# Converting a mixture's weights through a PSUM bank, with four word buffers

## The chip, the cores and the metric

The program runs on one core of a Trainium2 chip. Its engines are TensorE (PE, with its weight load PEld), VectorE (DVE), ScalarE (ACT), GpSimd (POOL) and SyncE (SP), which here issues nearly all input DMAs. The metric is the device time of one execution in microseconds (us): 1005.35 is the median of three runs before (1004.15 to 1005.42).

## The reference

Three layers in a row. A windowed attention: 4 batches, 8 heads, 768 positions of 64; a query sees the 128 positions up to its own and the first 4. A dense layer with three gates, and a routed layer of 8 experts:

```
x = softmax(where(keep, q@k.T/8, -1e9)) @ v          # then (3072, 512)
h = max(max(x@w1, x@w2), x@w3)                       # w*: (512, 768)
y = h @ w_out                                        # (768, 512)
out[tokens of e] = relu(y[tokens] @ u1[e]) @ u2[e]   # greedy routing, 384 tokens each
```

The weights w1, w2, w3, w_out come as 64-bit floats. All else is float32, and routing needs close to its full precision, so most products are computed from a high and a low part of each operand, in three matmuls.

## The kernel before

Work is cut into 8 groups of 384 tokens. A group needs four attention units (two heads each); the first 8 units, of groups 0 and 1, are "native", in plain float32. A unit is scores on PE (L123), copies and masks to a tile T (ACT L134, DVE L130 and L135 to L137), a row maximum (DVE L141), exponentials (ACT L144), a reciprocal and a scaling on POOL (L147), transposes on PE (L25), a mask product (DVE L163) and the product with v (PE L170, L172). A native unit needs key tiles with zeros in half of the partitions: `zeros` writes them (L53), into memory that the output weights take later.

`group` runs the first dense layer: six slices f of the hidden width, each 36 matmuls (L268, mm), whose maxima are taken by ACT and DVE (L270, L271) into hm; then a high and a low part of h are made (L275, L276). Group 0 is special: its slices are written to memory from hm (L278) and read back later by `reload`, which makes the parts again; the parts that `group` makes for it are not read.

The slices' weights must be converted first, 18 blocks of 128x512 for w1 to w3 and 6 for w_out. `single` loads 64-bit words into st (two buffers), DVE takes out bits of the low word into cA (L220), ACT scales the other word (L221), POOL adds the two (L222) and DVE puts in the sign and top bits (L223). `split` then makes the high part on ACT (L212) and the low part on POOL (L213). All of these tiles lie in SBUF. `load_w(f)` does this for the three blocks of one slice.

The order of each engine's instructions is fixed when the program is built, by a list scheduler that works with its own costs; the string `order` gives the sequence in which the units (a) and the weight slices (w) are offered to it. On the chip every engine runs its list in order, and a DMA queue does too.

Of the kernel before, what the change touches and what calls it, by code (L numbers as in the profile page):

```python
# [26 lines left out]
class Attn:  # L27
# [175 lines left out]
class Moe1:  # L203
    def __init__(s, tc, words,wgate, consts, wpool, main, conv, mm, pt, pss, ident):
        s.tc=tc; s.nc=tc.nc; s.mm=mm; s.pss=pss; s.main=main; s.conv=conv; s.ident=ident; s.consts=consts
        s.src=words; s.wgate=wgate
        s.W=[[wpool.tile([128,4,768],FR,name=f"w{i}{x}") for x in "hl"] for i in range(3)]
        s.WO=None; s.at=None
        s.WG=main.tile([128,6,16],FR,name="wgt")
    def split(s,src,hi,lo):  # L210
        nc=s.nc
        nc.scalar.activation(hi,src,AF.Copy)  # L212
        nc.gpsimd.tensor_tensor(lo,src,f32(hi),op=OP.subtract)  # L213
    def single(s,src):

        nc=s.nc
        st=s.conv.tile([128,512,2],I32,name="st",bufs=2)
        nc.sync.dma_start(st.rearrange("p n t -> p (n t)"),src.bitcast(I32))
        A=s.conv.tile([128,512],I32,name="cA",bufs=2); C=st[:,:,0]
        nc.vector.tensor_scalar(A,st[:,:,1],0x07ffffff,3,op0=OP.bitwise_and,op1=OP.logical_shift_left)  # L220
        nc.scalar.activation(C,st[:,:,0].bitcast(U32),AF.Copy,scale=2.0**-29)  # L221
        nc.gpsimd.tensor_tensor(A,A,C,op=OP.add)  # L222
        nc.vector.scalar_tensor_tensor(A,st[:,:,1],-0x40000000,A,op0=OP.bitwise_and,op1=OP.bitwise_or)  # L223
        return A.bitcast(FT)
    def load_w(s,f):
        for i in range(3):
            v=s.single(s.src[f*3+i]).rearrange("p (k n) -> p k n",k=4)
            s.split(v,s.W[i][0][:,:,f*128:(f+1)*128],s.W[i][1][:,:,f*128:(f+1)*128])
    def load_out(s,f):
# [17 lines left out]
        for x in range(2):  # L247
            nc.vector.tensor_copy(s.WO[x][:,f,:,256:260],f32(s.WG[:,f,8*x:8*x+8]).rearrange("p (u e) -> p u e",u=2))
    def group(s,xs,spill=None,pair=False,pool=None,mid=None,between=None):

        nc=s.nc; main=s.main
        X=[]
        for p in range(4):
# [4 lines left out]
            X.append((h,l))  # L258
        H=[]
        for f in range(6):  # L260
            if between is not None: between(f)
            m=main.tile([128,384],FT,name="hm",bufs=2)
            for i in range(3):
# [8 lines left out]
                if mid is not None and (f,i)==s.at: mid()  # L272
            h,l=((pool or main).tile([128,384],FR,name=f"h{x}{f}",bufs=1) for x in "hl")
            with s.tc.high_priority():
                nc.scalar.activation(h,m,AF.Copy)  # L275
                nc.vector.tensor_tensor(l,m,f32(h),op=OP.subtract)  # L276
            if spill is not None:
                for d,x in (zip(spill[f],(h,l)) if pair else ((spill[f],m),)): nc.sync.dma_start(d,f32(x))  # L278
            H.append((h,l))
# [243 lines left out]
class Moe2:  # L523

    def __init__(s,tc,w1,w2,x2d,out,wpool,act,main,mm,acc,pt,ident,nring):
        s.tc=tc; s.nc=tc.nc; s.w1=w1; s.w2=w2; s.x2d=x2d; s.out=out
        s.wp=wpool; s.act=act; s.main=main; s.ng=0; s.mm=mm; s.acc=acc; s.pt=pt; s.ident=ident; s.nring=nring
        s.scat=[]; s.n=-1
# [23 lines left out]
    def turn(s,xg,more=None):  # L552
# [9 lines left out]
        for d in range(4):  # L562
# [15 lines left out]
    def expert(s,X,ev,idx,mid=None):  # L578
# [9 lines left out]
        for f in range(F):  # L588
# [6 lines left out]
            h,l=(s.main.tile([128,384],FR,name=n%(4+f%2),bufs=1) for n in ("hh%d","hl%d"))  # L595
            with s.tc.high_priority():
# [13 lines left out]
def attention_mixtures(tc,q,k,v,vs,words,wg,u1,u2,out,off=60,spread=(0,1,3,4),native=8,order='a0 a0 a0 a0 w a1 a1 w w w w w a1 a1 a2',order1='a2 o o o o o o a2 a2',back=1,at=(1,0),s1=300,s2=400,nring=6):  # L610
    nc=tc.nc
    PS=bass.MemoryType.PSUM
    with ExitStack() as ctx:
# [19 lines left out]
        with tc.block(schedule_with_timeline_sim=True):  # L633
# [17 lines left out]
            for g in range(NG):  # L651
# [10 lines left out]
                if g==NG-1:  # L662
# [103 lines left out]
```

## Time and profile before

| | |
|---|---|
| median of 3 runs | 1005.35 us |
| profiled execution | 1004.42 us, of which its span is 1002.7 us |
| PE busy | 943.7 us, 94% |
| DVE, ACT, POOL busy | 711.8, 535.0, 343.5 us |
| mean granted clock of PE | 0.978 |

The busy share of PE is a mean over stages, so the stretches have to be read one by one. A busy PE is not a dense one: what a matmul costs in a row of matmuls is the distance between two starts, which is about half of the duration that its row shows.

### The profile page before, as it was taken

To read this page: it belongs to the slowest core of one execution; us is meant where nothing else is said; L and a number is where in the kernel's file an instruction comes from. 1 tells how busy PE (TensorE), PEld (TensorE's weight loads), DVE (VectorE), ACT (ScalarE), POOL (GpSimd) and SP (SyncE) were. 2 spreads that over 40 slices of the span, in tenths; PEclk is the share of its full clock that TensorE was granted. 3 is DMA by queue.
4 is the path that set the end of the run, shared out by engine and by line. 5 is a ranking of instruction groups with operands and counts; after the bars stand their busy time and mean duration, and the time that the engine had idled before them with its cause. 6 is when DMAs were issued, how large, how long until landed. Compare 5 with 4: busy or idle time off the path is not lost.

```text
span 1002.7 us, 18536 instructions
## 1 busy us (share of the span) xinstructions
PE 943.7 (94%) x6594; PEld 860.5 (86%) x6594; DVE 711.8 (71%) x1770; ACT 535.0 (53%) x1416; POOL 343.5 (34%) x307
## 2 busy tenths in 40 slices
PE   4879999979999999999999999989999999999996
PEld 3668899879999998998999998887888887888895
DVE  7988987787888875776754444887888988843320
ACT  5667664888878776677653211332433343454431
POOL 3687655044645435335433000011202111233331
PEclk9899999998999998999999999998999999999999
DMA  7444412231112111112210002542435443553430
GB/s 213 135 155 139 133 62 65 65 99 61 52 50 70 54 45 59 37 47 72 71 48 12 1 1 75 179 133 88 152 99 169 129 143 121 169 189 114 149 106 32
DMA packets 50541, 95.04 MB, mean 95 GB/s; under 512 B 6704, under 2 KB 20784, under 8 KB 50448
## 3 DMA queue, kind: packets, MB, share of 16 engines
q1 hardware_dynamic: 45312, 79.04, 25.5%
q0 software_dynamic: 3840, 12.45, 3.7%
q10 hardware_dynamic: 1296, 2.36, 0.6%
q8 instruction: 52, 0.85, 0.4%
q14 instruction: 41, 0.34, 0.1%
HBM read 77.84 MB, written 16.12 MB: 94 GB/s over the span
## 4 chain that ended last, share of the span: by engine, by line
PE 68%; DVE 13%; ACT 7%; issue 6%; DMA 4%; POOL 1%; POOLq 0%; DVEq 0%; SPq 0%; ACTq 0%
PE mm L268 24%; PE acc L587 11%; PE mm L594 11%; PE mm L291 6%; PE po L181 3%; PE rc L392 2%; PE pp L25 2%; DVE kz L95 1%; PE pt L25 1%; DMA sa<-in_u_dram 1%; PE ps L123 1%; DVE qs L97 1%; DMA st<-in_words_dram 1%; DMA sb<-in_u_dram 1%; DVE cA L223 1%
## 5 line engine op out<-in xcount | busy, mean ns | idle before, releaser
L177 POOL TENSOR_TENSOR L<-A_w,H 128x768 fp32r<-128x768 f32 x46 | 87.7, 1906 | 125.6 <-ACT H L176 101.2
L271 DVE TENSOR_TENSOR hm<-mm,hm 128x384 f32<-128x384 f32 x96 | 53.1, 553 | 53.9 <-PE mm L268 52.4
L549 POOL DMA_INDIRECT xg<-x2d,idx x24 | 25.5, 1063 | 188.5 <-PE mm L594 67.0
L537 ACT ACTIVATE wah<-sa 128x512 fp32r<-128x512 f32 x64 | 40.5, 632 | 89.6 <-PE mm L594 65.6
L537 ACT ACTIVATE wbh<-sb 128x512 fp32r<-128x512 f32 x64 | 40.4, 631 | 72.8 <-PE acc L587 61.5
L291 PE MATMUL mm<-woh,hh 128*128 128x260 f32 (+1 forms) x252 | 75.2, 300 | 4.2 <-DVE LG L294 4.2
L587 PE MATMUL acc<-wbh,hh 128*128 128x512 f32 x192 | 77.7, 404 | 0.0
L291 PE MATMUL mm<-woh,hl 128*128 128x260 f32 (+1 forms) x252 | 73.6, 296 | 4.2 <-DVE hl L308 2.7
L587 PE MATMUL acc<-wbh,hl 128*128 128x512 f32 x192 | 77.2, 402 | 0.0
L587 PE MATMUL acc<-wbl,hh 128*128 128x512 f32 x192 | 76.9, 401 | 0.0
L291 PE MATMUL mm<-wol,hh 128*128 128x260 f32 (+1 forms) x252 | 73.2, 292 | 0.0
L538 DVE TENSOR_TENSOR wbl<-sb,wbh 128x512 fp32r<-128x512 f32 x64 | 44.0, 688 | 35.0 <-ACT wbh L537 34.8
L268 PE MATMUL mm<-xh,w2h 128*128 128x384 f32 x192 | 67.3, 351 | 1.2 <-ACT hm L270 1.2
L268 PE MATMUL mm<-xh,w1h 128*128 128x384 f32 x192 | 67.0, 349 | 1.3 <-DVE hm L271 0.5
L268 PE MATMUL mm<-xh,w0h 128*128 128x384 f32 x192 | 66.9, 348 | 0.0
L268 PE MATMUL mm<-xl,w0h 128*128 128x384 f32 x192 | 65.3, 340 | 1.2 <-DVE xl L257 1.2
L268 PE MATMUL mm<-xl,w1h 128*128 128x384 f32 x192 | 65.5, 341 | 0.0
L268 PE MATMUL mm<-xh,w1l 128*128 128x384 f32 x192 | 65.3, 340 | 0.0
L268 PE MATMUL mm<-xl,w2h 128*128 128x384 f32 x192 | 65.3, 340 | 0.0
L268 PE MATMUL mm<-xh,w2l 128*128 128x384 f32 x192 | 65.2, 340 | 0.0
L268 PE MATMUL mm<-xh,w0l 128*128 128x384 f32 x192 | 64.7, 337 | 0.0
L598 DVE SCALAR_TENSOR_TENSOR hl<-mm,hh 128x384 fp32r<-128x384 f32 x64 | 35.3, 552 | 40.7 <-ACT hh L597 40.3
(315 smaller groups left out, 3087.1 us busy)
## 6 DMA issues: line engine op xcount, KB each, us to landing
sa<-in_u_dram SPq DMA_DIRECT2D x64, 256.0 KB
sb<-in_u_dram SPq DMA_DIRECT2D x64, 256.0 KB
st<-in_words_dram SPq DMA_DIRECT2D x24, 512.0 KB
qn<-in_q_dram SPq DMA_DIRECT2D x24, 192.0 KB
x2d<-xo SPq DMA_DIRECT2D x15, 256.0 KB
kn<-in_k_dram SPq DMA_DIRECT2D x12, 264.0 KB
vn<-in_v_dram SPq DMA_DIRECT2D x12, 256.0 KB
kn<-in_k_dram SPq DMA_DIRECT2D x12, 198.0 KB
```

The source lines that it names most:

```text
L25: nc.tensor.transpose(out,x,f32(ident))
L177: nc.gpsimd.tensor_tensor(L,Af,f32(H),op=OP.subtract)
L181: nc.tensor.matmul(po[:,q:q+n],u['VS'][:,blk,128*h:128*h+128],part[:,c:c+n],start=(part is H and j==0),stop=False,skip_group_check=True)
L268: nc.tensor.matmul(ps[:,:384],s.W[i][a][:,p,f*128:(f+1)*128],X[p][b],start=(n==0),stop=(n==11)); n+=1
L271: else: nc.vector.tensor_tensor(m,ps[:,:384],m,op=OP.max)
L291: nc.tensor.matmul(ps[:,:n],H[f][a][:,t*128:(t+1)*128],s.WO[b][:,f,u,:n],start=(k==0),stop=(k==17)); k+=1
L537: nc.scalar.activation(h,src,AF.Copy)
L538: (nc.gpsimd if s.n>=6 and nm=="wa" else nc.vector).tensor_tensor(l,src,f32(h),op=OP.subtract)
L549: nc.gpsimd.indirect_dma_start(out=g,out_offset=None,in_=s.x2d[0:first or 3072],in_offset=bass.IndirectOffsetOnAxis(ap=idx[:,t:t+1],axis=0 ...
L587: nc.tensor.matmul(acc[t],H[f][a][:,t*128:(t+1)*128],W[f][1][b],start=(f==0 and n==0),stop=(f==F-1 and n==2)); n+=1
L594: nc.tensor.matmul(ps[:,:384],W[f][0][a][:,k,:],X[k][b],start=(n==0),stop=(n==11)); n+=1
L598: nc.vector.scalar_tensor_tensor(l,ps[:,:384],0.0,f32(h),op0=OP.max,op1=OP.subtract)
```

## The change

`zeros` uses POOL in place of DVE. In `single` the bits of the low word go to a PSUM bank of the pool `ps`, which has three banks and also takes the scores; DVE then joins the top bits with them, into an SBUF tile R, and POOL adds the scaled word last. R is one of three tiles where A was one of two. For w1 to w3 (`ring`) the words go in turn to four buffers in one tile HL, which later holds the high and low parts of h and is used by group 0 for nothing else; w_out keeps the two buffers st. Group 0 writes hm to memory and makes no parts. Tiles that were single ones (hh0 to hl5) are slices of HL.

```diff
     def zeros(s,ts):
-        for h,t in enumerate(ts): s.nc.vector.memset((f32(t) if t.dtype==FR else t)[64-64*h:128-64*h],0.0)
+        for h,t in enumerate(ts): s.nc.gpsimd.memset((f32(t) if t.dtype==FR else t)[64-64*h:128-64*h],0.0)
...
-    def single(s,src):
+    def single(s,src,ring=False):
 
         nc=s.nc
-        st=s.conv.tile([128,512,2],I32,name="st",bufs=2)
+        if ring and s.stage is None: s.stage=s.main.tile([128,12,384],FT,name="HL").rearrange("p a b -> p (a b)").bitcast(I32)
+        if ring: st=s.stage[:,s.n%4*1024:(s.n%4+1)*1024].rearrange("p (n t) -> p n t",t=2)
+        else: st=s.conv.tile([128,512,2],I32,name="st",bufs=2)
         nc.sync.dma_start(st.rearrange("p n t -> p (n t)"),src.bitcast(I32))
-        A=s.conv.tile([128,512],I32,name="cA",bufs=2); C=st[:,:,0]
+        A=s.pss.tile([128,512],FT,name="ps").bitcast(I32); C=st[:,:,0]
+        if ring and s.n%3==2: R=s.stage[:,4096:4608]
+        else: R=s.conv.tile([128,512],I32,name="cA",bufs=2)
+        s.n+=1
         nc.vector.tensor_scalar(A,st[:,:,1],0x07ffffff,3,op0=OP.bitwise_and,op1=OP.logical_shift_left)
         nc.scalar.activation(C,st[:,:,0].bitcast(U32),AF.Copy,scale=2.0**-29)
-        nc.gpsimd.tensor_tensor(A,A,C,op=OP.add)
-        nc.vector.scalar_tensor_tensor(A,st[:,:,1],-0x40000000,A,op0=OP.bitwise_and,op1=OP.bitwise_or)
-        return A.bitcast(FT)
+        nc.vector.scalar_tensor_tensor(R,st[:,:,1],-0x40000000,A,op0=OP.bitwise_and,op1=OP.bitwise_or)
+        nc.gpsimd.tensor_tensor(R,R,C,op=OP.add)
+        return R.bitcast(FT)
+    def part(s,x,f):
+        return s.HL[:,"hl".index(x)*6+f]
...
         H=[]
+        if s.HL is None and spill is None: s.HL=main.tile([128,12,384],FR,name="HL")
...
-            h,l=((pool or main).tile([128,384],FR,name=f"h{x}{f}",bufs=1) for x in "hl")
+            if s.HL is None: nc.sync.dma_start(spill[f],m); continue
+            h,l=(pool.tile([128,384],FR,name=f"h{x}{f}",bufs=1) if pool else s.part(x,f) for x in "hl")
```

The scheduler then lists the work of the first half anew. The counts of the instructions are the same but for the ten memsets (from DVE to POOL) and six high and six low parts of 128x384 (gone from ACT and DVE). From the last slice of the seventh group's first layer on, PE's list is the same as before.

POOL near the start: T_w and wol are units' tiles T, vk_ and vns belong to a unit's first positions, cA and st (or HL) to the conversion. Before:

```order
L114 MEMSET T_w 128x264 x2
L114 MEMSET wol 128x264
L101 CAST vk_103<-vns 40x128
L102 TENSOR_TENSOR vk_103<-vns,vk_103 40x128
L101 CAST vk_107<-vns 40x128
L102 TENSOR_TENSOR vk_107<-vns,vk_107 40x128
L222 TENSOR_TENSOR cA<-cA,st 128x512 x2
L213 TENSOR_TENSOR w0l<-cA,w0h 128x4x128
L147 TENSOR_TENSOR T_w<-T_w,l 128x792
L222 TENSOR_TENSOR cA<-cA,st 128x512
L213 TENSOR_TENSOR w1l<-cA,w1h 128x4x128
```

In the changed kernel, where the eight memsets of L53 stand ahead of these rows:

```order
L114 MEMSET wol 128x264
L101 CAST vk_103<-vns 40x128
L102 TENSOR_TENSOR vk_103<-vns,vk_103 40x128
L101 CAST vk_107<-vns 40x128
L102 TENSOR_TENSOR vk_107<-vns,vk_107 40x128
L147 TENSOR_TENSOR T_w<-T_w,l 128x792
L114 MEMSET T_w 128x264
L101 CAST vk_103<-vns 40x128
L147 TENSOR_TENSOR T_w<-T_w,l 128x792
L102 TENSOR_TENSOR vk_103<-vns,vk_103 40x128
L147 TENSOR_TENSOR wol<-wol,l 128x792
L228 TENSOR_TENSOR cA<-cA,HL 128x512
```

The scalings (L147) of the first three units now stand in front of the first weight block (L228 is the addition, which was L222); before, two additions and a low part stood in front of the first scaling.

POOL later, where the weights of the fourth and fifth slices are made (w0l to w2l are the low parts). Before:

```order
L213 TENSOR_TENSOR w0l<-cA,w0h 128x4x128
L147 TENSOR_TENSOR wol<-wol,l 128x792
L213 TENSOR_TENSOR w1l<-cA,w1h 128x4x128
L222 TENSOR_TENSOR cA<-cA,st 128x512
L101 CAST vk_103<-vns 40x128
L222 TENSOR_TENSOR cA<-cA,st 128x512
L102 TENSOR_TENSOR vk_103<-vns,vk_103 40x128
L213 TENSOR_TENSOR w2l<-cA,w2h 128x4x128
L147 TENSOR_TENSOR T_w<-T_w,l 128x792
L114 MEMSET wol 128x264
L213 TENSOR_TENSOR w0l<-cA,w0h 128x4x128
L222 TENSOR_TENSOR cA<-cA,st 128x512
```

In the changed kernel:

```order
L101 CAST vk_107<-vns 40x128
L228 TENSOR_TENSOR HL<-HL 128x512
L213 TENSOR_TENSOR w1l<-cA,w1h 128x4x128
L228 TENSOR_TENSOR cA<-cA,HL 128x512
L102 TENSOR_TENSOR vk_107<-vns,vk_107 40x128
L213 TENSOR_TENSOR w2l<-HL,w2h 128x4x128
L228 TENSOR_TENSOR cA<-cA,HL 128x512
L213 TENSOR_TENSOR w0l<-cA,w0h 128x4x128
L228 TENSOR_TENSOR HL<-HL 128x512
L213 TENSOR_TENSOR w1l<-cA,w1h 128x4x128
L228 TENSOR_TENSOR cA<-cA,HL 128x512
L213 TENSOR_TENSOR w2l<-HL,w2h 128x4x128
```

Additions and low parts now follow each other almost without a unit's work between them.

PE, in the second slice of group 0's first dense layer (xh and xl are the parts of its tokens, w0h to w2l the weights, pt and pp transposes of a unit's T). Before:

```order
L123 MATMUL ps<-woh,qf 128x260 x3
L268 MATMUL mm<-xh_1043,w0h 128x384
L268 MATMUL mm<-xl_1044,w0h 128x384
L268 MATMUL mm<-xh_1043,w0l 128x384
L25 MATMUL pt<-ident,wol 128x128 x3
L25 MATMUL pp<-ident,wol 128x128 x3
L268 MATMUL mm<-xh_1047,w0h 128x384
L268 MATMUL mm<-xl_1048,w0h 128x384
L268 MATMUL mm<-xh_1047,w0l 128x384
L268 MATMUL mm<-xh_1051,w0h 128x384
L268 MATMUL mm<-xl_1052,w0h 128x384
L268 MATMUL mm<-xh_1051,w0l 128x384
```

In the changed kernel, in the same slice (L276 was L268):

```order
L276 MATMUL mm<-xh_1050,w1l 128x384
L276 MATMUL mm<-xh_1038,w2h 128x384
L276 MATMUL mm<-xl_1039,w2h 128x384
L276 MATMUL mm<-xh_1038,w2l 128x384
L276 MATMUL mm<-xh_1042,w2h 128x384
L276 MATMUL mm<-xl_1043,w2h 128x384
L276 MATMUL mm<-xh_1042,w2l 128x384
L276 MATMUL mm<-xh_1046,w2h 128x384
L276 MATMUL mm<-xl_1047,w2h 128x384
L276 MATMUL mm<-xh_1046,w2l 128x384
L276 MATMUL mm<-xh_1050,w2h 128x384
L276 MATMUL mm<-xl_1051,w2h 128x384
```

Slices of group 0 now follow each other, and the scores and transposes of the seventh unit on come later.

## Rows read from the trace of the kernel before

**Rows 1.** The page, part 1: busy us, share and instructions by engine.

```profile
PE 943.7 (94%) x6594; PEld 860.5 (86%) x6594; DVE 711.8 (71%) x1770; ACT 535.0 (53%) x1416; POOL 343.5 (34%) x307
```

**Rows 2.** Stretches: busy us of PE, PEld, DVE, ACT, POOL; PEclk; DMA share; GB/s.

```profile
0.00:75.00 75.00, 52.41 (x225) 38.92 (x225) 66.38 (x133) 46.32 (x164) 46.32 (x49) 0.91 0.55 167
...
117.00:200.00 83.00, 79.71 (x511) 77.14 (x510) 64.54 (x122) 53.46 (x142) 33.76 (x26) 0.99 0.23 72
...
545.00:1002.70 457.70, 439.29 (x3405) 386.15 (x3404) 288.95 (x962) 156.42 (x304) 74.99 (x71) 0.99 0.35 112
```

**Rows 3.** Shorter stretches, same columns.

```profile
20.00:30.00 10.00, 5.51 (x19) 4.46 (x19) 9.80 (x17) 7.12 (x26) 5.78 (x5) 0.67 0.66 202
...
50.00:75.00 25.00, 19.79 (x98) 15.47 (x94) 22.20 (x39) 16.57 (x59) 20.36 (x16) 0.93 0.49 155
```

**Rows 4.** Waits of PE, 0 to 75 us: total us, times, longest.

```profile
PE ps L123 <- DVE wol L135: 6.1, 3, 5.3
...
PE ps L123 <- DVE T_w L135: 4.8, 5, 2.0
```

**Rows 5.** Waits of the SP queue, 0 to 120 us, same columns.

```profile
SPq L218 <- DVE cA L223: 28.1, 13, 7.7
```

**Rows 6.** DVE by line, 0 to 170 us: busy us, mean ns, idle before.

```profile
L223 DVE SCALAR_TENSOR_TENSOR cA<-st,cA 128x512 int32<-128x512 int32 x24 | 28.4, 1181 | 1.3 <-POOL cA L222 1.2
L220 DVE TENSOR_SCALAR cA<-st 128x512 int32<-128x512 int32 x24 | 19.4, 811 | 2.5 <-DMA st<-in_words_dram 2.4
...
L163 DVE TENSOR_TENSOR A_w<-pp,ul 128x768 f32<-128x768 f32 x10 | 9.5, 950 | 1.7 <-PE pp L25 1.6
...
L276 DVE TENSOR_TENSOR hl<-hm,hh 128x384 fp32r<-128x384 f32 x9 | 8.3, 921 | 3.1 <-ACT hh L275 3.1
```

**Rows 7.** Line L223: ns min/median/max, first and last start in us.

```profile
L223 DVE SCALAR_TENSOR_TENSOR cA<-st,cA x24: 641/763/3184, 15.3 to 161.9; 128x512 int32<-128x512 int32 x24
```

**Rows 8.** Line L213, its third group, same columns.

```profile
L213 POOL TENSOR_TENSOR w2l<-cA,w2h x6: 1257/1284/1299, 30.4 to 115.7; 128x512 fp32r<-128x512 f32 x6
```

**Rows 9.** POOL by line, 0 to 170 us: busy us, mean ns, idle before.

```profile
L222 POOL TENSOR_TENSOR cA<-cA,st 128x512 int32<-128x512 int32 x24 | 34.0, 1420 | 17.4 <-DVE cA L220 7.8 <-ACT st L221 5.7 <-ACT m L142 1.8
L147 POOL TENSOR_TENSOR T_w<-T_w,l 128x792 f32<-128x792 f32 x7 | 11.5, 1646 | 1.3 <-DVE l L146 1.3
...
L102 POOL TENSOR_TENSOR vk<-vns,vk 40x128 fp32r<-40x128 f32 x12 | 7.6, 635 | 0.2
```

**Rows 10.** Timeline of DVE, 0 to 40 us: start us, us, instruction.

```profile
8.11 0.23 DVE L130 COPY_PREDICATED T_w<-ca,ps 128x128 f32<-128x128 uint8 x1
...
13.45 0.42 DVE L220 TENSOR_SCALAR cA<-st 128x512 int32<-128x512 int32 x1
...
32.19 1.98 DVE L220 TENSOR_SCALAR cA<-st 128x512 int32<-128x512 int32 x1
```

**Rows 11.** Timeline of POOL, 0 to 40 us, same columns.

```profile
1.04 0.56 POOL L114 MEMSET T_w<- 128x264 f32 x2
...
38.40 1.72 POOL L147 TENSOR_TENSOR wol<-wol,l 128x792 f32<-128x792 f32 x1 [1.47 <-DVE l L146]
```

**Rows 12.** Timeline of PE, 37 to 47 us, same columns.

```profile
37.90 0.89 PE L268 MATMUL mm<-xh,w0h 128*128 128x384 f32 x1
...
43.55 1.29 PE L172 MATMUL po<-wol,vnn 128*64 128x256 f32 x6
44.78 0.55 PE L25 MATMUL pp<-ident,wol 128*128 128x128 f32 x3
45.17 1.48 PE L123 MATMUL ps<-woh,qf 128*128 128x260 f32 x6
46.49 0.49 PE L25 MATMUL pp<-ident,wol 128*128 128x128 f32 x3
```

**Rows 13.** Timeline of PE, 100 to 120 us, same columns.

```profile
103.37 0.34 PE L268 MATMUL mm<-xh,w0h 128*128 128x384 f32 x1
103.55 0.33 PE L268 MATMUL mm<-xl,w0h 128*128 128x384 f32 x1
```

More of the change, by code (lines that the diff above doesn't have):

```diff
@@ L207, in __init__ @@
         s.W=[[wpool.tile([128,4,768],FR,name=f"w{i}{x}") for x in "hl"] for i in range(3)]
-        s.WO=None; s.at=None
+        s.WO=None; s.at=None; s.stage=None; s.HL=None; s.n=0
         s.WG=main.tile([128,6,16],FR,name="wgt")
@@ L248, in load_out, with group @@
             nc.vector.tensor_copy(s.WO[x][:,f,:,256:260],f32(s.WG[:,f,8*x:8*x+8]).rearrange("p (u e) -> p u e",u=2))
-    def group(s,xs,spill=None,pair=False,pool=None,mid=None,between=None):
+    def group(s,xs,spill=None,pool=None,mid=None,between=None):
         nc=s.nc; main=s.main
@@ L277, in group @@
             if spill is not None:
-                for d,x in (zip(spill[f],(h,l)) if pair else ((spill[f],m),)): nc.sync.dma_start(d,f32(x))
+                for d,x in zip(spill[f],(h,l)): nc.sync.dma_start(d,f32(x))
             H.append((h,l))
@@ L305, in reload @@
             nc.sync.dma_start(m,spill[f])
-            h=s.main.tile([128,384],FR,name=f"hh{f}",bufs=1); l=s.main.tile([128,384],FR,name=f"hl{f}",bufs=1)
+            h,l=s.part("h",f),s.part("l",f)
             nc.scalar.activation(h,m,AF.Copy)
@@ L523, with __init__ @@
 class Moe2:
-    def __init__(s,tc,w1,w2,x2d,out,wpool,act,main,mm,acc,pt,ident,nring):
+    def __init__(s,tc,w1,w2,x2d,out,wpool,act,main,mm,acc,pt,ident,nring,part):
         s.tc=tc; s.nc=tc.nc; s.w1=w1; s.w2=w2; s.x2d=x2d; s.out=out
-        s.wp=wpool; s.act=act; s.main=main; s.ng=0; s.mm=mm; s.acc=acc; s.pt=pt; s.ident=ident; s.nring=nring
+        s.wp=wpool; s.act=act; s.main=main; s.ng=0; s.mm=mm; s.acc=acc; s.pt=pt; s.ident=ident; s.nring=nring; s.part=part
         s.scat=[]; s.n=-1
@@ L570, in turn @@
                     nc.tensor.matmul(p[:,t*128:(t+1)*128],xg[t][:,d*128:(d+1)*128],f32(s.ident),start=False,stop=True,skip_group_check=True)
-            b=("xh%d","xl%d") if s.ng%2==0 else ("hh%d","hl%d")
-            h,l=(s.main.tile([128,384],FR,name=n%d,bufs=1) for n in b)
+            h,l=(s.main.tile([128,384],FR,name=f"x{x}{d}",bufs=1) if s.ng%2==0 else s.part(x,d) for x in "hl")
             nc.scalar.activation(h,p[:,:384],AF.Copy)
@@ L594, in expert @@
                     nc.tensor.matmul(ps[:,:384],W[f][0][a][:,k,:],X[k][b],start=(n==0),stop=(n==11)); n+=1
-            h,l=(s.main.tile([128,384],FR,name=n%(4+f%2),bufs=1) for n in ("hh%d","hl%d"))
+            h,l=(s.part(x,4+f%2) for x in "hl")
             with s.tc.high_priority():
@@ L666, in attention_mixtures @@
                     r=Route(tc,LG,rt,rw,rc)
-                H6,H=H if g==NG-1 else None,M.group(xs[g],sp if g==0 else sp2 if g==NG-3 else None,g>0,hp if g==NG-1 else None,rest,between)
+                H6,H=H if g==NG-1 else None,M.group(xs[g],sp if g==0 else sp2 if g==NG-3 else None,hp if g==NG-1 else None,rest,between)
                 while late: between(spread[0])
@@ L677, in attention_mixtures @@
         wp=P("wp",1,side="right"); act=P("act",1,side="right")
-        E=Moe2(tc,u1,u2,x2d,out,wp,act,main,mm,acc,pst,A.ident,nring)
+        E=Moe2(tc,u1,u2,x2d,out,wp,act,main,mm,acc,pst,A.ident,nring,M.part)
         def step(n):
@@ L690, in keep @@
             if not K7:
-                for i in range(4): K7[i]=tuple(main.tile([128,384],FR,name=f"h{x}{i}",bufs=1) for x in "hl")
+                for i in range(4): K7[i]=M.part("h",i),M.part("l",i)
             b=4*t+d
```

2 lines of the change are left out of this document (1 added, 1 removed).

## The prediction

> **What bounds the kernel now.** I read the busy shares first, then stretches, then waits, then single timelines. PE is busy 94% of the span [rows 1], so a gain must come from its idle time or from time at a lower clock. The stretches say where these are: in the first 75 us PE is busy for 52.4 us at a clock of 0.91, and in the 458 us from 545 on it loses 18.4 us [rows 2]. PE's list of instructions is unchanged from about there, so that loss stays. In the first 75 us DVE is busy for 66.4 us, 89%: it, and not PE, sets the pace there. PE's longest waits in this stretch are for DVE's masks L135, 6.1 and 4.8 us [rows 4]. The granted clock is 0.67 from 20 to 30 us, where PE was busy for 5.5 us of 10, and 0.93 from 50 to 75 us [rows 3]. The SP queue waits 28.1 us, in 13 waits, for L223 to give back one of two word buffers [rows 5]. So weights come late because DVE is late, and the next words are fetched only when it is done.
>
> Why DVE is late: L223 takes 0.641 us at its fastest and 3.184 at its slowest [rows 7], and 1.18 in the mean, L220 0.81 [rows 6], while the first L220 took 0.42 and another one 1.98 [rows 10]. Its twin is POOL, which adds and subtracts in SBUF meanwhile. L163, with one operand in PSUM, is flat at 0.95 for 768 elements [rows 6].
>
> The Trainium skill (SBUF — State Buffer, "Who interferes with whom") says that a VectorE instruction with two SBUF inputs, or in a two-port mode, shares a port with GpSimd's reads and that one blocks the other, while one with at most one SBUF input outside these modes does not. The spread of L223 against the flat L163 agrees.
>
> **The change part by part.** All sums are made against the profiled execution, 1004.42 us (span 1002.7 and 1.7 around it); the median of the runs lies 0.93 above it.
>
> Conversion on DVE. Before, a pair costs 0.81 + 1.18 = 1.99 us. No row shows DVE writing to PSUM. By length from L163 an instruction of 512 elements with a PSUM operand takes 0.95 x 512/768 = 0.63, and it cannot be above 0.95; I take 0.68, and 1.36 for the pair. The ends for the pair are 0.42 + 0.64 = 1.06 and 1.99, no gain at all. By my value the 24 pairs give back 24 x 0.63 = 15 us of DVE, 11 of them before the last of the 18 blocks of w1 to w3.
>
> The rule that speaks against this is in the Trainium skill (VectorE: DVE Perf Modes, "Why PSUM operands drop a tier"): an fp32 operand in PSUM caps VectorE at one element per cycle, so L220 would lose its fast form. The fastest rows, 0.42 for L220 and 0.64 for L223, look like two rates for 512 elements and agree. By the rule both instructions would take about the 0.64 of L223, 1.3 us for the pair, which is inside my bounds.
>
> Memsets. Two of 128x264 took 0.56 us on POOL from 1.04 us on [rows 11], 0.28 each, so eight of twice the length take 4.5 us by estimate (4 to 5) and the three of L114 behind them end at about 6.4. The first mask L130 starts at 8.11 us [rows 10], held by DVE's own memsets. It can now start at about 6.4 us: 1.7 us earlier, and DVE has eight instructions less. What is queued behind POOL's memsets is the first vk copies, which wait for their input and are needed only by the first L170.
>
> First weights. Nine conversion instructions stand in DVE's list between the first masks and the third unit's scaling, 0.42 us the first and 1.98 the last, 7.4 us in sum [rows 10]. They now stand behind that unit's reciprocal. The third unit's scaling, at 38.40 us before [rows 11], starts at about 38.4 - 7.4 - 1.7 = 29.3. But the first weight block waits for it on POOL: three blocks and a scaling later the first slice's matmuls can start at about 34 us, against 37.90 [rows 12]. Here only 4 us are won.
>
> Pace of weights. Before, the 18 low parts end at 115.7 + 1.3 = 117 us [rows 8], which from the first L220 at 13.45 is 5.75 us for a block. Now four buffers hold the words ahead, and DVE needs 1.36 us and not 1.99. POOL is what is late next: 1.42 for the addition before (1.30 undisturbed, by the same length as L213's 1.28) and 1.28 for the low part [rows 8, 9], 2.6 us in sum. From 31 us on it does 18 x 2.6 = 47, three scalings of 1.65 = 5, and five pairs of small vk instructions of about 1.1 = 5.5 (0.635 for the second of a pair) [rows 9]. The last low part ends at 31 + 57.5 = 88.5 us without any wait; I allow 1.5 us, so 90, and PE is done with the slice at 92.
>
> What PE has done by then: 216 first-layer matmuls 0.175 apart [rows 13] = 37.8 us, and six units of about 4.5 us (six scores 1.32, three transposes 0.39 three times, v products 1.23 [rows 12], and two L170 of 384 columns, 0.65 by the length of the scores), with the scores of two more: 67 us. Before, the fifth slice starts at 103.37 us [rows 13], where 144 of these matmuls and nearly nine units are behind it: 62 us. The same 67 us are reached at about 109. So PE is 17 us ahead at that point.
>
> Given back. The order has only moved units: the seventh and part of the eighth and ninth come after the weights and not before. They put about 10 us of DVE work into the next stretch, where DVE is busy for 64.5 of 83 us and PE idles for 3.3 [rows 2]. DVE has room for that on paper, at 90%; I take half of it, 5 us, as new idle time of PE.
>
> Small parts. The six low parts not made are 6 x 0.92 = 5.5 us of DVE [rows 6], in slices where PE is fed, so they count only as cover for the 10 us above. The PSUM bank that a block holds for some 1.5 us is one of three that scores use; where a score waits for it PE has first-layer matmuls in its list only behind that score, and I count 0 to 3 us, taken within the 5. In the SP queue two more word loads now stand ahead of the fifth unit's keys and q; 1.05 MB at the 202 GB/s of that stretch [rows 3] are 5.2 us, in a queue that waits less for buffers, for a unit whose scores PE reaches only with the first slice, after 30 us: nothing.
>
> Sum: 1004.4 - 17 + 5 = 992.4, with the 0.93 of the median 993.
>
> **The rivals.** *POOL starves PE (slower).* PE's list now has five slices in a row with few units between, and POOL makes their weights. In favour: POOL has no slack there, and its additions wait for ACT and DVE in their fixed order. With a block every 3.35 us the last would end at 31 + 10.5 + 60.3 = 102, PE would be done with the slice at 104 and 5 us ahead, and the moved units take these back: from that pace on the change loses. At 4.5 us a block it ends at 122.5, PE is 15 us behind, and the time is 1004.4 + 15 + 5 + 0.9 = 1025. Against it: the old pace had a cause, the buffers, that goes.
>
> *PSUM gives nothing.* If the pair stays at 1.99 us, 11 us of DVE return before the last weight; with half on the path, 998.
>
> *Nothing is given back.* If DVE's relief covers the moved units, the whole 17 us and up to 6 us of lower clock (a third of 5.5 us, and 7% of 19.8 us, and the like behind them) stay: 984.
>
> *All is swallowed.* PE's later waits grow by as much as it was early, since other engines' lists are newly mixed up to 545 us: 1004 to 1006.
>
> **How the numbers follow.** My forecast has 0.55, nothing given back 0.17, PSUM giving nothing 0.12, all swallowed 0.07, starvation 0.09. The range, 982 to 1004, takes in all but the starved case and the ends of the others. Less than 0.2%, 2 us, cannot be told from no change by these runs: faster 0.84, same 0.07, slower 0.09.
>
> **What would show it.** L220's follower at 0.6 to 0.75 us with a narrow spread, the same for L223's; the first mask before 7 us; the last w2l low part near 89 us where it was at 115.7; DVE's busy time below 60 us in the first 75; the clock of that stretch above 0.91; the stretch from 545 us on as long as before. I am wrong if PE's waits for ACT's or POOL's weight parts in the first 90 us exceed 10 us, or if the stretch behind the last weights grows by more than 10.

## The result, and the profile after

The changed kernel is slower: 1020.4 us in the median of four runs (1019.36 to 1024.98) against 1005.38 beside them, a ratio of 1.0148 [1.0122, 1.0173]. The prediction, 993 and faster, was wrong. The profiled span is 1018.1 us, 15.4 longer, at a mean granted clock of 0.966, before 0.978; the four runs have 0.961 to 0.970, the longest run the lowest. One of the twelve runs with the words on ACT, below, took 1294.96 us at a clock of 0.652 and stands in no ratio.

The page, part 1, answers to [rows 1]: PE is busy for 7 us more and idle for 9 more, while DVE has 28 us less to do.

```profile
PE 950.5 (93%) x6594; PEld 865.4 (85%) x6594; DVE 684.2 (67%) x1754; ACT 533.7 (52%) x1410; POOL 342.3 (34%) x317
```

The stretches of [rows 2], same columns. From 545 us on PE idles for 17.6 us, where it was 18.4; the loss lies ahead of that.

```profile
0.00:75.00 75.00, 54.96 (x253) 39.88 (x254) 52.36 (x115) 45.18 (x156) 39.93 (x53) 0.91 0.58 176
117.00:200.00 83.00, 74.42 (x470) 69.60 (x470) 57.30 (x129) 52.51 (x148) 37.33 (x36) 0.94 0.21 64
545.00:1018.10 473.10, 455.53 (x3511) 402.17 (x3509) 296.69 (x975) 162.25 (x314) 81.58 (x76) 0.99 0.34 109
```

The two DVE instructions of the conversion (L225 was L220, L227 was L223), ns min/median/max, answer to [rows 7]; the last low part to [rows 8]. The conversion is flat now, but the last low part starts at 108.2 us, only 7.5 earlier.

```profile
L225 DVE TENSOR_SCALAR ps<-HL x18: 673/684/698, 32.0 to 98.8; 128x512 int32<-128x512 int32 x18
...
L227 DVE SCALAR_TENSOR_TENSOR cA<-HL,ps x12: 674/678/689, 32.7 to 99.9; 128x512 int32<-128x512 int32 x12
...
L213 POOL TENSOR_TENSOR w2l<-HL,w2h x6: 1266/1296/1302, 45.4 to 108.2; 128x512 fp32r<-128x512 f32 x6
```

Two shorter stretches of before (same columns as above), where the order of units and slices changes:

```profile
80.00:120.00 40.00, 38.21 (x215) 33.39 (x214) 38.00 (x64) 27.64 (x84) 30.30 (x29) 0.96 0.44 141
120.00:160.00 40.00, 38.82 (x248) 37.38 (x247) 32.32 (x48) 23.79 (x56) 24.69 (x20) 1.00 0.26 86
```

And of after:

```profile
80.00:120.00 40.00, 37.45 (x200) 34.30 (x199) 24.42 (x46) 19.66 (x56) 25.42 (x22) 0.96 0.31 106
120.00:160.00 40.00, 32.69 (x191) 28.68 (x191) 29.55 (x60) 28.57 (x88) 18.66 (x18) 0.87 0.20 63
```

Once the slices are used up, from 120 to 160 us, PE does 191 matmuls where it did 248, and its clock is granted at 0.87 in the mean: from 130 to 140 us PE is busy for 5.9 us of 10, and from 140 to 150 us the granted clock is 0.61, mostly the lower of its two levels, 1.2 GHz. The outputs of units 7 and 8 (the eighth native one is number 8) are copied at 125 and 135 us, not at 101 and 117. Their scores start at 100.8 and 109.7 us, not at 59.3 and 71.0: they now stand behind the weight blocks. The first starts right behind the instruction that frees the bank of the 17th of the 18 weight blocks (start us, us, instruction):

```profile
99.90 0.69 DVE L227 SCALAR_TENSOR_TENSOR cA<-HL,ps 128x512 int32<-128x512 int32 x1 [0.40 <-POOL w1l L213]
100.75 0.60 PE L123 MATMUL ps<-woh,qf 128*128 128x260 f32 x2
```

Their products with v (L172, from 122.5 us) come behind the sixth slice.

The measure of progress below is therefore not a slice but the count of matmul records (one for each matmul in the trace) up to 188 us: 893 before, 852 after. At 6.5 records a us (1371 in the 210 us from 250 us of before) 41 records are 6.3 us. In the table, "slice 6" and "groups" are the starts of the last maximum of a first layer; "behind at 188" is the missing records in us; "late" is the growth from 188 us to the end of group 7, that end less 609 and less "behind", rounded at the end. The runs below were on other chips, on which the kernel before took 1006 to 1015 us; the ratio is to it on the same chip, and the columns of us, which end at 626, are compared with the trace of [rows 1]. A run of the same list (one tile) is within 1.5 us of that trace in all columns. What differs by chip lies behind group 7: that stretch takes 394 us before and 392 after on the first chip, and 395 to 406 in the runs below. Each row of us is one execution, and executions of one kernel on one chip differ by 2 to 11 us, so a difference of 1 or 2 us between rows says little.

| run | slice 6 | group 1 | 3 | 5 | 7 | behind at 188 | late | ratio |
|---|---|---|---|---|---|---|---|---|
| before | 138 | 188 | 373 | 518 | 609 | 0 | 0 | 1 |
| after | 117 | 192 | 387 | 533 | 626 | 6.3 | 10 | 1.0148 |
| units first | 126 | 180 | 379 | 525 | 617 | -4.6 | 12 | 1.0067 |
| own bank | 134 | 190 | 370 | 515 | 620 | 4.8 | 6 | 1.0127 |
| add in SBUF | 137 | 188 | 382 | 526 | 618 | 0.5 | 8 | 1.0091 |
| two buffers | 121 | 201 | 392 | 538 | 630 | 13.8 | 8 | 1.0197 |
| no splits | 133 | 183 | 383 | 529 | 621 | -6.0 | 18 | 1.0101 |
| zeros | 136 | 189 | 384 | 531 | 622 | 1.4 | 12 | 1.0092 |
| one tile | 137 | 188 | 374 | 519 | 610 | -0.2 | 1 | 1.0005 |
| PSUM alone | 121 | 201 | 397 | 540 | 631 | 13.8 | 8 | 1.0191 |
| list alone | 137 | 191 | 386 | 532 | 623 | 3.4 | 11 | 1.0089 |
| old list, full | 142 | 194 | 381 | 527 | 619 | 5.8 | 4 | 1.0046 |
| old list, SBUF | 141 | 195 | 379 | 523 | 614 | 6.0 | -1 | 1.0052 |
| units far ahead | 144 | 198 | 390 | 536 | 628 | 10.3 | 8 | 1.0143 |
| stores on ACT | 144 | 195 | 380 | 526 | 617 | 6.2 | 2 | 1.0069 |
| words on ACT | 140 | 193 | 379 | 526 | 617 | 4.3 | 4 | 1.0062 |
| both on ACT | 141 | 194 | 378 | 522 | 614 | 5.2 | -1 | 1.0037 |
| SBUF, stores on ACT | 139 | 193 | 379 | 524 | 615 | 4.3 | 2 | 1.0056 |
| twice, full | 152 | 204 | 388 | 534 | 627 | 18.0 | 0 | 1.0221 |
| twice, before | 141 | 193 | 384 | 528 | 620 | 4.8 | 6 | 1.0131 |

### The profile page after: what moved, and what is told of

It reads as the page before. It is cut to its first block, busy times and chain, and to the rows that moved or that the text cites. A ratio compares the mean times of both kernels' runs of the same rounds, so it can differ in the third digit from the quotient of the medians.

```text
span 1018.1 us, 18536 instructions
## 1 busy us (share of the span) xinstructions
PE 950.5 (93%) x6594; PEld 865.4 (85%) x6594; DVE 684.2 (67%) x1754; ACT 533.7 (52%) x1410; POOL 342.3 (34%) x317
## 4 chain that ended last, share of the span: by engine, by line
PE 74%; DVE 8%; ACT 6%; issue 5%; DMA 4%; POOL 1%; SPq 0%; POOLq 0%; ACTq 0%; DVEq 0%
PE mm L276 28%; PE acc L595 10%; PE mm L602 10%; PE mm L300 7%; PE po L181 3%; PE rc L401 2%; PE pp L25 2%; DMA sa<-in_u_dram 2%; PE pt L25 1%; PE ps L123 1%; DMA HL<-in_words_dram 1%; PE po L172 1%; PE acc L329 1%; PE ps L126 1%; PE ps L127 1%
## 5 line engine op out<-in xcount | busy, mean ns | idle before, releaser
L595 PE MATMUL acc<-wbh,HL 128*128 128x512 f32 x384 | 134.4, 404 | 0.0
L300 PE MATMUL mm<-woh,HL 128*128 128x260 f32 (+1 forms) x432 | 94.2, 307 | 4.8 <-DVE HL L317 1.9
L595 PEld LDWEIGHTS acc<-wbh,HL 128*128 128x128 f32 x384 | 71.9, 189 | 14.3 <-ACT wah L546 1.5
L300 PEld LDWEIGHTS mm<-woh,HL 128*128 128x128 f32 x432 | 75.6, 207 | 6.8 <-DVE LG L303 2.5
L595 PE MATMUL acc<-wbl,HL 128*128 128x512 f32 x192 | 77.0, 401 | 0.0
L276 PE MATMUL mm<-xh,w0h 128*128 128x384 f32 x192 | 67.3, 351 | 4.3 <-DVE hm L279 2.2
L276 PE MATMUL mm<-xl,w0h 128*128 128x384 f32 x192 | 66.0, 344 | 5.1 <-DVE xl L264 5.1
L602 PE MATMUL mm<-HL,wah 128*128 128x384 f32 x256 | 67.9, 344 | 0.0
L276 PE MATMUL mm<-xh,w1h 128*128 128x384 f32 x192 | 66.4, 346 | 0.8 <-ACT hm L278 0.5
L276 PE MATMUL mm<-xh,w2h 128*128 128x384 f32 x192 | 66.8, 348 | 0.1
L276 PE MATMUL mm<-xh,w0l 128*128 128x384 f32 x192 | 66.0, 344 | 0.0
L276 PE MATMUL mm<-xh,w2l 128*128 128x384 f32 x192 | 65.9, 343 | 0.0
L276 PE MATMUL mm<-xh,w1l 128*128 128x384 f32 x192 | 65.6, 342 | 0.0
L276 PE MATMUL mm<-xl,w2h 128*128 128x384 f32 x192 | 65.6, 341 | 0.0
L276 PE MATMUL mm<-xl,w1h 128*128 128x384 f32 x192 | 65.3, 340 | 0.0
L300 PE MATMUL mm<-wol,HL 128*128 128x260 f32 (+1 forms) x216 | 64.2, 299 | 0.0
```

Source lines behind the costliest of these rows:

```text
L276: nc.tensor.matmul(ps[:,:384],s.W[i][a][:,p,f*128:(f+1)*128],X[p][b],start=(n==0),stop=(n==11)); n+=1
L300: nc.tensor.matmul(ps[:,:n],H[f][a][:,t*128:(t+1)*128],s.WO[b][:,f,u,:n],start=(k==0),stop=(k==17)); k+=1
L595: nc.tensor.matmul(acc[t],H[f][a][:,t*128:(t+1)*128],W[f][1][b],start=(f==0 and n==0),stop=(f==F-1 and n==2)); n+=1
```

## The experiments

**What holds the units back.** Theory A: the PSUM bank does, since banks of `ps` are handed out in the order of the program, and all blocks of weights stand ahead of units 7 and 8 in `order`. Theory B: the words and their buffers do the harm. Theory C: any new list of the scheduler loses in the later groups. The first run has units 7 and 8 written ahead of four weight slices:

```diff
-order='a0 a0 a0 a0 w a1 a1 w w w w w a1 a1 a2'
+order='a0 a0 a0 a0 w a1 a1 w a1 a1 w w w w a2'
```

> The changed kernel with the last two native units offered to the scheduler behind the second slice and not behind the sixth (order a0 a0 a0 a0 w a1 a1 w a1 a1 w w w w a2); all else stays, the shared bank too. Theory A: their scores get banks ahead of four slices' blocks and PE has units between the slices: 990 to 1005. Theory B: 1012 to 1022, and theory C: 1008 to 1022.

Measured 1.0067 [1.0041, 1.0093]. The outputs of units 7 and 8 are copied at 96 and 108 us, and the kernel is 4.6 us ahead at 188: the 0.8% won back is A's part. 12 us are then lost, so that the time (1012 us, put on the first chip) lies in C's range and not in A's.

The conversion with a PSUM bank of its own, and two for the scores:

```diff
-        A=s.pss.tile([128,512],FT,name="ps")...
+        A=s.pcv.tile([128,512],FT,name="pc")...
-pss=A_("pss",3,space=PS)
+pss=A_("pss",2,space=PS); pcv=A_("pcv",1,space=PS)
```

> The changed kernel, but a block's low bits go to a PSUM bank of a pool of their own (one bank), and the scores keep two banks of three. Theory A (banks): the blocks of all six slices stand ahead of units 7 and 8 in the program and take the shared pool's banks in that order, so these units' scores come after the weights, PE finds no unit to do between 85 and 130 us, and what was won is lost twice. With a bank of their own PE's list has unit 7 again after the second slice: the seventh unit's output near 80 us (89 in the changed kernel for the eighth's forerunner, 73 for the sixth), 995 to 1008 us. Theory B (words): four word loads in the queue and 512 KB blocks behind spills delay the units' inputs: unchanged here, 1015 to 1023. Theory C (any new list costs about this much after 200 us, whatever units 7 and 8 do): 1010 to 1022.

1.0127 [1.0100, 1.0154]. The units come back (110 and 125 us), but two score banks change the list most of all (PE's order is that of before only from 584 us on); inconclusive by itself.

The conversion in SBUF with POOL's add in the middle, as before, all else changed:

```diff
-        A=s.pss.tile([128,512],FT,name="ps")...
...
-        nc.vector.scalar_tensor_tensor(R,...,A,...)
         nc.gpsimd.tensor_tensor(R,R,C,op=OP.add)
+        nc.vector.scalar_tensor_tensor(R,...,R,...)
```

> The changed kernel with the conversion in SBUF in the old sequence (VectorE, GpSimd's addition, VectorE), so no PSUM bank is taken; four word buffers, three result tiles, zeros on GpSimd and no unused parts stay. Theory A: units 7 and 8 stand between the slices as before the change, and the four buffers still help: 993 to 1004. VectorE's pair is back near 1.8 us. Theory B (the four buffers and their word loads do the harm): 1012 to 1022. Theory C: 1008 to 1020.

1.0091 [1.0057, 1.0125]. Without the bank the units are back and nothing is lost by 188 us, and still 8 us are lost behind it. A is half of the story at most.

The changed kernel with two word buffers, and two result tiles in place of three:

```diff
-            v=s.single(s.src[f*3+i],True)...
+            v=s.single(s.src[f*3+i])...
```

> The changed kernel with two word buffers and two result tiles for all blocks, as before the change; the PSUM bank stays shared. Theory A: units 7 and 8 stay behind the weights, 1012 to 1024. Theory B: the harm goes with the buffers, 998 to 1006. Theory C: 1008 to 1022.

1.0197 [1.0164, 1.0229]: B falls. The four buffers, with the third result tile, help, by 0.5%.

**One part of the change at a time, on the kernel before.** Theory D is that the single tile HL makes waits of its own.

```diff
+            if spill is not None and not pair: nc.sync.dma_start(spill[f],m); continue
```

> The kernel before, with one thing changed: the hidden values of the first group are sent to memory at once, without being split into high and low parts that nobody reads (12 instructions of ACT and DVE fewer of some 7,700). By theory A (the PSUM bank of the conversion holds units 7 and 8 behind the slices, and that is the whole loss) this is not slower: 1.000, between 0.997 and 1.002. By theory C (any new list of the scheduler costs something in the later groups, since the constants of the kernel before were chosen on its own list) it is 1.004 to 1.009 slower, and the ground is lost between 188 and 460 us, where the list has unit 10 some 2 us later than before. Theory D (the single tile for the halves of H makes false waits) says 1.000 as well.

1.0101 [1.0066, 1.0136]: twelve instructions that nobody needs are left out, the kernel is 6 us ahead at 188 us, and loses 18 after that.

```diff
-        ... s.nc.vector.memset(...)
+        ... s.nc.gpsimd.memset(...)
```

> The kernel before, with one thing changed: the 20 memsets of the half-zero tiles are on POOL and not on DVE. Theories A and D: between 0.996 and 1.002 (the first scores 1 to 2 us earlier at best). Theory C: 1.004 to 1.009, with the loss between 188 and 460 us.

1.0092 [1.0059, 1.0126]. A and D cannot explain either; C does. (By the trace it is ten memsets.)

```diff
-            h,l=((pool or main).tile([128,384],FR,name=f"h{x}{f}",bufs=1) for x in "hl")
+            h,l=(pool.tile([128,384],FR,name=f"h{x}{f}",bufs=1) if pool else s.part(x,f) for x in "hl")
```

> The kernel before, with one thing changed: the twelve high and low halves of H are parts of one tile and no longer twelve tiles. PE's list has the same order as before. Theory D (a write to one part of the tile waits for readers of another part, which the order of the list does not show): 1.004 to 1.010, with ACT or DVE waiting for PE ahead of the lines that write H. Theories A and C: the same list, so 1.000, between 0.998 and 1.002.

1.0005 [0.9982, 1.0028]: D falls for the parts of h. That the words lie in the same tile is not in this run.

```diff
-        nc.gpsimd.tensor_tensor(A,A,C,op=OP.add)
-        nc.vector.scalar_tensor_tensor(A,...)
+        nc.vector.scalar_tensor_tensor(R,...,A,...)   # A in a bank of ps
+        nc.gpsimd.tensor_tensor(R,R,C,op=OP.add)
```

> The kernel before, with one thing changed: the conversion goes through a PSUM tile of the scores' pool (two word buffers as before, splits and zeros as before). Theory A: this alone has units 7 and 8 behind all six slices (attention results 6 and 7 come after slice 5 in PE's list) and carries the whole loss: 1.012 to 1.020, as the run with two buffers (1.020) did. Theory C: 1.004 to 1.009, like any other new list. The rival from the prediction that PSUM gives nothing: 1.000.

1.0191 [1.0159, 1.0223]. The bank alone puts units 7 and 8 at 135 and 152 us and 13.8 us are gone at 188: A shown for the early part, C's 8 us on top.

**The list by itself.** The kernel before, the order string alone altered as in the first run:

```diff
-order='a0 a0 a0 a0 w a1 a1 w w w w w a1 a1 a2'
+order='a0 a0 a0 a0 w a1 a1 w a1 a1 w w w w a2'
```

> The kernel before with no instruction changed, only the order string (a0 x4, w, a1, a1, w, a1, a1, w, w, w, w, a2). Up to unit 9 PE's list has everything within 1 us of PE's work of its old place; from unit 10 on it is the list that the run with the zeros on POOL had (its last 4,750 instructions of PE, from group 2's second half, are those of before again). Theory C: 1.006 to 1.010, as that run (1.0092), lost between 188 and 460 us. If the list is harmless and the edits do it: 1.000, within 0.002.

1.0089 [1.0061, 1.0118]. No instruction differs, and 0.9% is lost: C is shown for this list. The stretch from 188 us to the end of group 7 (columns as above), of before and then of this run:

```profile
188.00:609.10 421.10, 405.67 (x2686) 394.45 (x2685) 290.14 (x588) 273.66 (x776) 161.66 (x137) 0.98 0.16 49
188.00:623.30 435.30, 411.22 (x2708) 399.33 (x2707) 297.51 (x598) 276.88 (x793) 159.94 (x136) 0.98 0.15 48
```

The stretch is 14.2 us longer (in the longest of its six runs, 3 us above their median). 3.4 us are the 22 matmuls that were behind at 188, and PE idles 8.7 us more, at the same clock. From 188 to 460 us PE's waits for other engines sum to 21.1 us there, against 14.3; the two largest with the new list:

```profile
PE ps L126 <- DVE T_x L135: 4.5, 3, 2.2
PE pp L25 <- DVE A_w L163: 4.1, 4, 2.0
```

They are waits of the attention units, where before the largest was for the logits of the output layer.

In the changed kernel only half of the loss is of this kind. Its stretch, and that of the run at 1.0221 below, whose list is another again:

```profile
188.00:625.70 437.70, 416.82 (x2727) 405.16 (x2725) 296.84 (x611) 282.26 (x805) 162.55 (x136) 0.96 0.16 48
188.00:627.20 439.20, 421.15 (x2802) 408.46 (x2801) 304.93 (x628) 287.90 (x819) 169.01 (x142) 0.99 0.16 49
```

The changed kernel's stretch is 16.6 us longer. 6.3 us are the 41 records that were behind, and PE idles 5.5 us more. The other 5 us go with the clock: what was done took PE that much longer, at 0.96 and not 0.98. The run at 1.0221 idles 2.6 us more than before and gets as much back at 0.99, so that its "late" is 0.

Not every row is another list. By the traces PE's order is the same in list alone, zeros and add in SBUF from 260 us on, and in units first from 363 us on. Own bank, PSUM alone, no splits, two buffers and the changed kernel have other orders and lose 6 to 18 us behind 188. And PE's order in list alone is that of before from 547 us on, which is later than the expectation says.

The converse: the whole change with a string for which PE's list behind unit 9 is that of before.

```diff
+order='a0 a0 a0 a0 w a1 w a1 a1 w w a1 a2 w w'
```

> The whole change, every instruction of it, with one string altered: units and weights are written in the order a0 x4, w, a1, w, a1, a1, w, w, a1, a2, w, w. That gives PE a list whose last 7,082 of 7,737 instructions are word for word those of the kernel before (ACT's last 967, DVE's last 1,464 too), with units 6 and 7 within 4 us of PE's work of their old places; only what stands ahead of unit 9 differs. Theory C (the loss is in the scheduler's list, not in the edits): 0.990 to 0.998, since the words still come earlier, and no ground is lost between 188 and 460 us. If the edits themselves slow the later groups (zeros on POOL, the one tile for H, splits left out): 1.004 to 1.010, as the run with the units first (1.007).

1.0046 [1.0021, 1.0072], slower than expected; by its time it lies in the rival's range. Behind 188 us 4 us are lost and not 10, as C has it, and PE idles there for 16.0 us, before 15.4, so that the edits do not slow the later groups by waits. But 19 us ahead after the fourth slice (102 us, before 121) it is 4 behind after the sixth. By records it is only 2.6 us ahead at 120 us (488 against 471): units stand behind the fourth slice in this string.

The same for the run with the add in SBUF:

```diff
+order='a0 a0 a0 a0 w a1 a1 w a1 a1 w w w w a2'
```

> As the run with the conversion back in SBUF and POOL's add in the middle (four word buffers, splits left out, zeros on POOL; 1.0091), with one string altered: the order a0 x4, w, a1, a1, w, a1, a1, w, w, w, w, a2. Its first part has nearly the same order as there (units within 2 us of PE's work), its last 7,082 instructions of PE are those of the kernel before. Theory C: 0.997 to 1.001, all of the 0.9% of that run gone. If the edits cost the 0.9%: 1.007 to 1.010 again.

1.0052 [1.0028, 1.0075]: nothing is lost behind 188 us, 6 us are ahead of it. The time lies in neither range. C's sign is right twice, its numbers for the whole are not.

```diff
+order='a0 a0 a0 a0 w a1 a1 w a1 a1 a2 w w w w',order1='a2 o o o a2 o o o a2'
```

> The whole change with the units far ahead: order a0 x4, w, a1, a1, w, a1, a1, a2, w x4, and the first of the output weights moved too. Units 6 to 8 stand 4, 9 and 0 us of PE's work ahead of their old places, units 10 to 15 up to 9 us ahead; the last 5,744 of PE's 7,737 instructions are those of before. Theory C: little lost behind 250 us, so 0.994 to 1.003. If the edits cost: 1.007 to 1.012.

1.0143 [1.0113, 1.0174], a miss: 10 us behind at 188, where units had been moved ahead of slices. 8 us more are lost behind it; PE's order is that of before from 395 us on.

**SP's queue.** In the run at 1.0046 SP waited 20.4 us up to 145 us for slices that it was to store, with words behind these stores:

```profile
SPq L281 <- DVE hm L279: 20.4, 6, 4.9
```

```diff
-            if s.HL is None: nc.sync.dma_start(spill[f],m); continue
+            if s.HL is None: nc.scalar.dma_start(spill[f],m); continue
```

> The whole change with the list of before behind unit 9 (the run at 1.0046), and one thing altered: the six stores of the first group's hidden values are issued on ACT's queue, not on SP's, so that no words stand behind a store that waits for its slice. Theory E (the early gain is lost on SP's queue: in that run PE was 19 us ahead after the fourth slice and 4 behind after the sixth, with SP waiting 20 us at these stores): the sixth slice ends at 118 to 132 and not at 142, group 1 at 180 to 188, and the time is 0.990 to 0.998. Rival F (the words would come no earlier, since ACT's and DVE's own order and the units set the pace): sixth slice at 138 to 143, 1.003 to 1.006.

1.0069 [1.0042, 1.0096], sixth slice at 144 us, with PE's order the same in every record of the trace.

```diff
-        nc.sync.dma_start(st...,src...)
+        (nc.scalar if ring else nc.sync).dma_start(st...,src...)
```

> The same kernel (1.0046) with the loads of the words on ACT's queue and the stores where they were. Theory E: the words wait for a free buffer alone; sixth slice at 118 to 132, 0.990 to 1.000, less sure than the run with the stores on ACT since ACT then waits for POOL's adds itself. Rival F: 1.003 to 1.008.

1.0062 [1.0044, 1.0081], at 140. Both of these edits:

> Both on ACT's queue, the six stores and the loads of the words. Theory E: as the better of the two, 0.990 to 0.999. Rival F: 1.003 to 1.008.

1.0037 [1.0018, 1.0055], at 141; the best version found, still slower than before. The first edit on the run with the add in SBUF and the old list:

> The run with the conversion in SBUF and the list of before (1.0052), with the six stores on ACT's queue. Theory E: its words too stood behind the stores (SP waited 14 us there), so 0.998 to 1.002, with the sixth slice at 130 to 138 and not at 141. Rival F: 1.004 to 1.006.

1.0056 [1.0034, 1.0077], at 139. Theory E falls, F stands, for kernels with the list of before; the changed kernel's own list was not run so.

**Is the conversion on the path?** DVE's first operation on a block, written twice:

```diff
         nc.vector.tensor_scalar(A,st[:,:,1],0x07ffffff,3,...)
+        nc.vector.tensor_scalar(A,st[:,:,1],0x07ffffff,3,...)
```

> The kernel of the run at 1.0046 (the whole change, list of before), with the first of DVE's two operations on each block of words written twice: 24 more operations of 0.68 us on DVE, 21 of them ahead of 150 us, some 14 us. It no longer has the list of before behind unit 9, so by theory C up to 0.9% comes on top, lost behind 188 us; the test is where the sixth slice and group 1 end (142 and 194 us in the run at 1.0046). Theory G (up to there the chain of the attention units sets the pace, and the conversion lies beside it): 138 to 146 and 190 to 199, time 1.005 to 1.015. Theory H (DVE's time for the conversion is on the path, as the prediction took it): 152 to 158 and 204 to 210, time 1.016 to 1.030.

1.0221 [1.0188, 1.0253]; sixth slice at 152 us, group 1 at 204, and 117 records, 18 us, behind at 188, 12 more than without it. Its granted clock up to 188 us is 0.88, without it 0.95, so that a part of the 12 us comes by way of the clock. DVE by line up to 150 us:

```profile
L225 DVE TENSOR_SCALAR ps<-HL 128x512 int32<-128x512 int32 x18 | 12.2, 683 | 1.7 <-DMA HL<-in_words_dram 1.7
L226 DVE TENSOR_SCALAR ps<-HL 128x512 int32<-128x512 int32 x18 | 12.1, 683 | 0.0
```

With the one `st` block, 12.8 us of DVE were added, and 12 came out as time: H, for the changed kernel.

> The kernel before with the same operation written twice, there 0.81 us in the mean: 24 more, 22 of them ahead of 150 us, some 18 us of DVE, which is busy for 108 of the first 120 us. Its list behind unit 9 is another too (up to 0.9% by theory C); the test is again the end of the sixth slice and of group 1 (138 and 188 us). Theory G: 136 to 144 and 186 to 195, time 1.003 to 1.013. Theory H: 150 to 156 and 202 to 208, time 1.018 to 1.032. A split result (before slower by 12 us or more, the changed kernel not) would say that the conversion did bound the kernel before and does not bound the changed one.

1.0131 [1.0094, 1.0168]; sixth slice at 141, group 1 at 193, 4.8 us behind at 188. Up to 150 us:

```profile
L224 DVE SCALAR_TENSOR_TENSOR cA<-st,cA 128x512 int32<-128x512 int32 x20 | 23.1, 1156 | 0.8 <-POOL cA L223 0.7
L220 DVE TENSOR_SCALAR cA<-st 128x512 int32<-128x512 int32 x20 | 12.9, 644 | 1.8 <-POOL w2l L213 1.3 <-DMA st<-in_words_dram 0.4
L221 DVE TENSOR_SCALAR cA<-st 128x512 int32<-128x512 int32 x20 | 10.3, 515 | 0.3
```

The three rows sum to 46.3 us, against 39.3 for the two of before in that stretch: 7 us were added and not the 18 expected, since the first operation got shorter (0.64 from 0.81). The sixth slice, group 1 and, within the interval, the time lie in G's ranges and not in H's. But 5 us did come out, and with 7 us added the run cannot tell G from H. So DVE's time for the conversion is shown to be on the path in the changed kernel, and for the kernel before it stays open.

## Why the prediction was wrong

- *Conversion on DVE*: right. 0.68 for each operation, flat, as taken; the spread of [rows 7] is gone. The rule of the Trainium skill (SBUF — State Buffer, "Who interferes with whom") agrees: with one operand of L227 in PSUM it no longer varies with what POOL does (0.674 to 0.689), while L264, which reads two SBUF tiles, takes 1.51 in the mean up to 170 us, 0.67 before. So does the Trainium skill in "Why PSUM operands drop a tier" (VectorE: DVE Perf Modes): L220's 0.42 is gone, at no cost in sum.
- *Memsets*: right in time, the first mask at 6.2 us; PE's first scores then wait 4.8 us for POOL's memsets and not 5.4 for q. *First weights*: the third unit's scaling starts at 32.8 us, not at 29.3, and the first slice at 36.6, not at 34.
- *Pace of weights*: the first step that failed. The last low part was to end at 88.5 us "without any wait" and ends at 109.5. In its five steps from 45.4 us a block takes 62.8/15 = 4.2 us, not 3.2. POOL comes to the blocks at 34.4 us and not at 31. From then on it works for 54.1 us, where the sum had 57.5, so the work was right; its waits, for which 1.5 us were allowed, are 20.8. The largest:

```profile
POOL vk L101 <- PE po L170: 8.4, 4, 6.8
POOL w1l L213 <- ACT w1h L212: 4.4, 2, 2.3
POOL HL L228 <- DVE HL L227: 3.3, 1, 3.3
```

  One is a unit's small copy in POOL's own list, which waits 6.8 us for PE to be done with the tile vk, with weights queued behind it. ACT's high parts (8.1 us in all) and DVE's L227 (4.3) come late in turn: from 31 to 110 us DVE waits 8.0 us and ACT 9.8 for words. The prediction counted SP's queue, which issues them in order, as free of cost. Up to 120 us SP waits at the word loads for 19.5 us and no longer for 35.7, but its waits in all are 86 us in both kernels; larger now are those for v tiles and for slices to store:

```profile
SPq L79 <- PE po L172: 22.1, 6, 7.6
SPq L281 <- DVE hm L279: 17.3, 3, 8.0
```

  With the list of before, words and stores on ACT's queue brought the sixth slice forward by 2 us at most, so that this queue is not shown to be the cause.
- *17 us ahead*: failed with it. The slices are 20 us ahead at the sixth, but that is work moved, not won: up to 120 us PE has 481 matmul records against 471, 1.5 us. The working also misread [rows 13]: 103.37 us is the start of the fourth slice (108 matmuls of L268 stand ahead of it), and the fifth starts at 118.55. Read rightly, the same working promises a larger lead, so this slip did not make the forecast too good.
- *Given back*: the step that turned the sign. I took 5 us, from DVE's room on paper. From 10 records ahead at 120 us the kernel falls to 41 behind at 188, 7.8 us: units 7 and 8, held behind the PSUM banks of the blocks, run with no slices beside them. PE idles for 7.3 of these 68 us, before for 1.6, while a unit passes from engine to engine, and its granted clock is 0.92, before 1.00. DVE had room (29.6 busy of 40 us) and it did not help. The small part on the PSUM bank, 0 to 3 us, had seen a score wait for a bank, and not that two units move behind the weights.
- *The later list*: missing from the sum. 10 us more are lost from 188 us to the end of group 7, with a list that the change did not mean to touch: 5.5 us as idle time of PE and 5 at a lower clock. I had this only as a rival, "all is swallowed", with 0.07 and without a loss beyond the gain. Three runs, of two lists, show 0.9 to 1.0% with hardly any instruction or none changed, and six with the old list have -1 to 4 us of it.
- The rival *POOL starves PE* names about the time that came, 1025, but not the way: POOL does wait for ACT and DVE, but PE's waits for weight parts in the first 90 us are not among its larger ones, and the slices were early.
- My condition for being wrong, a stretch behind the last weights that grows by more than 10 us, is what happened: from the sixth slice to the end of group 1 it is 75 us and was 51. Of the signs, DVE's first 75 us came true (52.4 us busy); the clock there stayed at 0.91.

In the prediction's terms: 1004.4 - 1.5 (ahead at 120 us) + 7.8 (given back) + 10.4 (later list) - 1.2 (behind group 7) = 1019.9, and the profiled execution took 1019.85. The units held behind a PSUM bank are shown to cost the early part; that a new list alone costs as much as the later part is shown, and so is that the old list takes most of that part away.

There is a gain under it. With the same order string as units first, which is 4.6 us ahead at 188, the kernel with no edit (list alone) is 3.4 behind, and the one with all but the PSUM conversion (old list, SBUF) 6.0 behind. How much of that is the conversion is not shown, since each of these has a list of its own, and leaving out the splits alone put the kernel before 6.0 ahead. It is less than a list can take away.

Open: which of the moved instructions costs the 0.9% behind 188 us; what in the changed kernel's list brings its lower clock; and why the runs with the old list are 4 to 6 us behind at 188.

## What to carry to other kernels

Where a scheduler lists the work, run a null edit first (another order string, a dead instruction left out): here it costs 0.9%, where the whole change was forecast to give 1.2%. Before a PSUM pool gets a new user, look which tiles are handed out behind it, for they wait in the program's order. Count all matmuls done by a time, not the ones that the edit makes early: filler used up early leaves the units without cover later. And set the granted clock beside the idle time: half of a loss can lie there.

## What the runs showed of the hardware

L220, which reads and writes SBUF, has a median of 0.43 us and a mean of 0.81: the long ones, up to 1.98, make the mean. With PSUM on one side it takes 0.68 (L225, which writes PSUM), and so does the second operation, which reads one operand from PSUM (L227).
